# Attention and product-key experts in one kernel: an output-weight load left out at the end, totals stored together, key copies and weight residuals moved to other engines, scores ahead of products

## The chip, the cores and the metric

The kernel runs on one core of a Trainium2 chip, as a single program. The engines are TensorE (PE in the profile, with weight loads as PEld), VectorE (DVE), ScalarE (ACT), GpSimd (POOL) and SyncE (SP); SP does no arithmetic here and issues most of the transfers. Each engine works through its own instructions in order, and waits at semaphores for the others. The metric is the device time of one execution in microseconds (us).

## The reference

With 2048 tokens of width 512, the output is `x + A(xn) + B(xn)`, where `xn` is the layer norm of `x`:

```python
def _A_ref(x, wq, wk, wv, wo):          # 32 query heads of width 16, one key and one value head
    q = (x @ wq).reshape(B, S, H, Dh)   # then heads first
    k, v = x @ wk, x @ wv
    p = softmax(einsum("bhqd,bkd->bhqk", q, k) * Dh ** -0.5)
    return einsum("bhqk,bkd->bhqd", p, v) ... @ wo

def _B_ref(x, w_q, k1, k2, u, v):       # 32 heads, 64 x 64 = 4096 experts, K = 2
    q1, q2 = halves of einsum("nd,dhc->nhc", xf, w_q)
    s1, s2 = q1 @ k1.T, q2 @ k2.T       # 64 scores each
    # top 2 of each, the 4 sums, the best 2 of these: experts and softmax gates g
    act = gelu(einsum("nd,nhkd->nhk", xf, u[top_e]))
    return einsum("nhk,nhk,nhkd->nd", g, act, v[top_e])
```

## The kernel before

**Tiling.** Tokens lie in 16 tiles of 128, four tiles to a group, four groups (0 to 3). Matrix products that must be exact to about fp32 use two-part operands: a rounded high part and a residual (`TERMS`, three matmuls for each product).

**The start** (`project_kv`, `project_q` and what calls them, lines 1183 to 1233). SP loads the first group's `x`, the query weights `wq` (L1187), the first expert weights (L469) and the next groups' `x` (L141, tile `xp`). For each group: VectorE takes means and variances (`norm_group`, L148 to L165, with a square root on ACT at L153), TensorE transposes (L180), ACT copies the high part out of PSUM (L181) and VectorE subtracts for the residual (L182). `wqs` holds the query weights' two parts: ACT makes the high part (L1202), GpSimd the residual (L1203). `project_kv` gives keys and values (L198), copied by ACT (L201), split by VectorE (L203, L204); the keys go into `kaug` at two base partitions, six small transfers for each group (L207 to L209) on ACT's queue. `project_q` makes four blocks of queries for each group (L227): ACT takes the high part (L231), VectorE the residual (L232), ACT the square (L234), TensorE a sum over heads (L235), and SP stores both parts to DRAM (L237, L238). The query parts have four buffers, so a new one waits for an older one's store.

Among this stand the first items of the expert scores: `wp_make` folds the experts' query weights with the key tables (products `pw`, L485; copies L486; transposes `pwt`, L492; copies and residuals L494, L495), and `item` multiplies them with the tokens (`psc`, L530: 12 matmuls for each token tile); VectorE finds maxima and their places (L543, L545), and `batch` turns four tiles' results into expert numbers and gates (L570 to L607, an exponential on ACT at L582). `gathers` then has GpSimd fetch the experts' rows (L964). The order in this part is made by a planner, which takes the program's order and its own durations. The start ends with a flag (`guard`, L262) that every engine reads before a branch.

**The main loop** (lines 1235 to 1306) has its order written out by hand. It runs 280 steps, `d` from 0 to 279, with `i = 2 * d`; 512 attention steps lie in the first 256, and the rest finishes what is under way. A step (`att_steps`) takes scores of one 128-key block against 4 heads (L325), the exponential on ACT (L328) into `pt`, and the products with the values two blocks later (L339). Between these, `run_scores` feeds in pieces of the expert scores up to a budget (`spent` counts their cost; a product `pw` counts 0.9), VectorE makes dot products with gathered rows (`dot`, L976) and weighted sums into `xa` (`add`, L1011). Groups 2 and 3 take the experts densely (`dense`: L723, L807, L848, L851). At step 0 `run_scores` runs first, with a budget of 6.0, which covers the whole of `wp_make`.

**The end.** `experts_out` puts a finished total's store on SP's list, one in each step (L1291, L1292), for the store at L448. `load_wo` loads the output weights into two gather buffers: at L1177 for each 128 steps, and at step 502 for the last block. The last block's attention output goes through `last_out_a` and `last_out_b` (L407, L415), is added to the totals that were read back (L418) and stored from SP and ACT (L419).

```python
        if i >= 128 and i % 128 == 10 or i == STEPS - 10:      # L1177
            load_wo()
```

Of the kernel before, what the change touches and what calls it, by code (L numbers as in the profile page):

```python
# [18 lines left out]
OP = mybir.AluOpType  # L19
# [10 lines left out]
NT = S // P  # L30
# [10 lines left out]
NGB = 12  # L41
# [14 lines left out]
def tile_kernel(ctx, tc, x, wq, wkv, wo, wqT, kT, uv, ub, vb, out):  # L56
    nc = tc.nc
# [11 lines left out]
    raw = lambda ap: ap.bitcast(F32)  # L69
# [122 lines left out]
    def project_kv(g):  # L192
        p = stile("pkv")[:, 0, :]
        n = 0
        for k in range(KC):
            for a, b in TERMS:
                w = (wkv_h, wkv_l)[a]
                nc.tensor.matmul(p[:32, :], w[:, k, :], XT[g][k][:, b, :], start=n == 0, stop=n == 11)  # L198
                n += 1
        kv = big.tile([32, 512], F32, name="kv", tag="wk", bufs=NWK)  # L200
        nc.scalar.copy(kv, p[:32, :])  # L201
        kh = big.tile([32, 2, 512], F32R, name="kh", tag="wk", bufs=NWK)
        nc.vector.tensor_copy(kh[:, 0, :], kv)  # L203
        nc.vector.tensor_tensor(out=kh[:, 1, :], in0=kv, in1=kh[:, 0, :], op=OP.subtract)  # L204
        c = slice(g * 512, (g + 1) * 512)
        for base in (0, 64):
            nc.scalar.dma_start(raw(kaug[base:base + 16, c]), raw(kh[:16, 0, :]))  # L207
            nc.scalar.dma_start(raw(kaug[base + 16:base + 32, c]), raw(kh[:16, 1, :]))
            nc.scalar.dma_start(raw(kaug[base + 32:base + 48, c]), raw(kh[:16, 0, :]))  # L209
        sq = start.tile([16, 512], BF16, name="ksq", tag="sq", bufs=2)  # L210
        nc.vector.tensor_mul(sq, kv[:16, :], kv[:16, :])
        nc.tensor.matmul(ksq_p[32 * g:32 * g + 32, :], blk[:16, 0:1].to_broadcast([16, 32]), sq,
                         start=True, stop=True)
        pt = xtile("pv_t")
        for c in range(GT):
            nc.tensor.transpose(pt[:, 32 * c:32 * c + 32], kv[:, c * P:(c + 1) * P], ident[:32, :32])
        nc.vector.tensor_copy(vaug[:, GT * g:GT * g + GT, :DH],
                              pt[:, :P].rearrange("p (c n) -> p c n", n=32)[:, :, DH:])
# [799 lines left out]
    def gathers(most):  # L1018
        while g_next[0] < NSL and g_next[0] < a_next[0] + NGB - lent[0] and most > 0:
            gather(g_next[0])  # L1020
            g_next[0] += 1
            most -= 1
# [107 lines left out]
    def att_steps(d, mid, fill):  # L1130
        i = 2 * d
        run(STORES)
        if 144 <= i < STEPS and i % 128 == 16:
            PWO.extend((i // 128 - 1, j) for j in range(4))
        if i < STEPS:
            u, kc = divmod(i, 16)
            if i == 0:
                load_q(0, rows=False)
                run_scores(until=spent[0] + 6.0)
            if kc == 4 and u + 1 < 32:  # L1140
                load_q(u + 1)
            scores(u, kc, 0)
            scores(u, kc, 1)
        if 0 < i <= STEPS:
            pu, pk = divmod(i - 2, 16)
            pv(pu, pk)
            pv(pu, pk + 1)
            if pk == 14:
                unit_tail(pu)
        mid()  # L1150
        if i < STEPS:
            scores(u, kc + 1, 0)
            scores(u, kc + 1, 1)
        if out_ready() and (i % 128 >= HOLD and PWO[0][0] != 1 or i % 4 == 0 and PWO[0][0] == 1):
            block_out()
            spent[0] += 3.6
        fill()

        pp, r = divmod(i, 32)
        if pp and pp < 16:  # L1160
            if r == 4:
                pair_load(pp - 1)
            if r == 6:
                pair_invert(pp - 1)
            if r == 10:
                pair_spread(pp - 1)
            if r == 12:
                pair_tail(pp - 1)
        if i == STEPS - 4:
            for j in range(3):  # L1170
                last_out_a(j)
        if i == STEPS + 2:
            last_out_a(3)
            last_out_b()
        if i >= 124 and i % 128 == 124 or i == STEPS - 30:
            lent[0] = 2
        if i >= 128 and i % 128 == 10 or i == STEPS - 10:  # L1177
            load_wo()
        if i == STEPS - 6:
            load_last()  # L1180
# [18 lines left out]
    for i in range(2):  # L1199
        for k in range(2):  # L1200
            w = start.tile([P, 2, 512], F32R, name="wqs", tag="wqs", bufs=4)
            nc.scalar.copy(w[:, 0, :], wraws[i][:, k, :])  # L1202
            nc.gpsimd.tensor_tensor(out=w[:, 1, :], in0=wraws[i][:, k, :], in1=w[:, 0, :], op=OP.subtract)  # L1203
            wqs.append(w)
    project_kv(0)
    norm_group(1, xs[1])
# [11 lines left out]
    transpose_group(2)  # L1218
    project_kv(2)
    xs.append([load_x(3 * GT + j, False) for j in range(GT)])  # L1220
    gathers(NGB)
    project_q(2, wqs)
    norm_group(3, xs[3])
    transpose_group(3)
    project_kv(3)
    project_q(3, wqs)
    run(STORES)
    start_stack.close()
# [6 lines left out]
    with tc.manual_schedule(engines={E_.PE, E_.Activation, E_.DVE, E_.Pool, E_.SP}):  # L1235
# [3 lines left out]
        for d in range(half + 24):  # L1239
# [11 lines left out]
            def mid():  # L1251
# [26 lines left out]
                def go():  # L1278
# [9 lines left out]
                        if rest:  # L1288
                            rest.pop(0)()
                    gathers(4)  # L1290
                    if OUTS:  # L1291
                        experts_out(OUTS.pop(0))  # L1292

                if dense_on[0] == 2:
                    POST_FILL.append(go)
# [58 lines left out]
```

## Time and profile before

| | |
|---|---|
| three timed runs | 1969.92, 1976.40 and 1984.79 us (median 1976.4) |
| the profiled execution's own time | 1972.45 us |
| its span, first to last instruction | 1970.7 us |
| mean granted TensorE clock | 0.975 |
| moved by DMA | 492.16 MB, mean 250 GB/s |
| software (gather) queue, share of 16 DMA engines | 41.2% |
| SP's and ACT's queues, share | 34.0% and 0.3% |

The page gives each engine's busy time over the span, with idle time put down to what ended it. An idle engine that nobody waits for costs nothing, so the busy shares say where to look, and the stretch at hand says what an edit is worth. Three kinds of rows are used below. A row of stretches has the stretch, its length, busy time and instruction count of PE, PEld, DVE, ACT and POOL, the granted clock, the DMA engines' share and GB/s. A row in order of time has start, length, engine, line, operation, output and inputs, and in brackets the idle time before it and what ended that. A row of waits has who waited for whom, us in total, how often, and the longest.

### The profile page before, as it was taken

The page shows a single profiled execution, that of the slowest core. Times are in us where ns is not written, and L with a number is a line of the kernel's source. Part 1 is how long each engine was busy: PE and PEld are TensorE (multiplying, and loading weights), DVE is VectorE, ACT ScalarE, POOL GpSimd, SP SyncE. Part 2 cuts the span into 40 slices and gives each one's busy share as a digit, 9 for nine tenths or more (in the row PEclk, how much of TensorE's full clock was granted, in tenths as well). Part 3 has the DMA queues.
Part 4 walks back from the last instruction along what each step waited for, and adds up shares of the span by engine and source line. Part 5 has one row for each costly group of instructions (what it writes and reads, how often), then busy time and mean ns, then how long its engine had stood idle before and what let it go on. Part 6 is the DMA issues. An engine that isn't in the chain of part 4 may idle for free.

```text
span 1970.7 us, 34755 instructions
## 1 busy us (share of the span) xinstructions
PE 1874.1 (95%) x10990; PEld 998.1 (51%) x10990; DVE 1679.4 (85%) x6713; ACT 1292.3 (66%) x1801; POOL 575.1 (29%) x540
## 2 busy tenths in 40 slices
PE   6879999999999998999999999999999989999997
PEld 3544444555555443555555445555554545555552
DVE  6626888899999975899999789999999769999993
ACT  3326666655557885788778555555578767778773
POOL 2201323222221222344344332222213215444430
PEclk9989999999999898999999999999999899999999
DMA  7756878787773676698889978877646858899982
GB/s 271 281 202 223 297 267 287 274 297 259 249 229 119 214 227 211 211 291 290 273 277 306 351 271 275 277 237 260 204 135 227 267 169 277 278 286 279 294 265 80
DMA packets 234201, 492.16 MB, mean 250 GB/s; under 512 B 93204, under 2 KB 93460, under 8 KB 234012
## 3 DMA queue, kind: packets, MB, share of 16 engines
q0 software_dynamic: 73728, 268.47, 41.2%
q1 hardware_dynamic: 158280, 219.82, 34.0%
q10 hardware_dynamic: 2004, 1.61, 0.3%
q8 instruction: 88, 1.44, 0.3%
q14 instruction: 101, 0.83, 0.1%
HBM read 428.46 MB, written 56.07 MB: 246 GB/s over the span
## 4 chain that ended last, share of the span: by engine, by line
PE 65%; DVE 18%; DMA 4%; ACT 2%; issue 2%; SPq 1%; another core or an unknown queue 0%; ACTq 0%; DVEq 0%
PE pv L339 18%; PE sc L325 13%; PE psc L530 10%; PE pout L848 9%; PE pact L723 9%; DVE i L545 5%; DVE m L543 3%; DVE xa L1011 3%; PE pg L807 3%; DVE g L976 2%; ACT pt L328 2%; PE pw L485 1%; PE pwo L432 1%; DMA dg<-gst 1%; DMA wqt<-in_wqT_dram 1%
## 5 line engine op out<-in xcount | busy, mean ns | idle before, releaser
L328 ACT ACTIVATE pt<-sc 128x1024 f32<-128x1024 f32 x1024 | 993.2, 1025 | 461.3 <-PE sc L325 392.6
L964 POOL DMA_INDIRECT g<-in_uv_dram,idx x512 | 561.9, 1097 | 1333.1 <-DVE xa L1011 724.1
L339 PE MATMUL pv<-pt,vaug 128*32 128x512 f32 x4096 | 511.1, 617 | 0.0
L325 PE MATMUL sc<-qa,kaug 64*128 64x512 f32 x2048 | 389.0, 454 | 26.6 <-ACT pt L328 25.8
L530 PE MATMUL psc<-wk,xt 128*128 128x512 f32 x1536 | 391.3, 402 | 5.9 <-DMA wk<-dw 2.1
L1011 DVE SCALAR_TENSOR_TENSOR xa<-g,w,xa 128x512 f32<-128x512 f32 x512 | 374.0, 750 | 0.1
L976 DVE CUSTOM_DVE_ANT_0 g<-g,xa 128x512 f32<-128x512 f32 x512 | 337.0, 687 | 7.4 <-DMA g<-in_uv_dram,idx 7.4
L530 PEld LDWEIGHTS psc<-wk,xt 128*128 128x128 f32 x1536 | 279.3, 189 | 110.7 <-issue 42.6
L325 PEld LDWEIGHTS sc<-qa,kaug 64*128 64x128 f32 x2048 | 157.6, 186 | 347.9 <-ACT pt L328 225.2
L339 PEld LDWEIGHTS pv<-pt,vaug 128*32 128x32 f32 x4096 | 109.2, 111 | 255.4 <-issue 253.8
L545 DVE FIND_INDEX8 i<-m,psc 128x8 uint32<-128x64 f32 x1024 | 207.5, 231 | 0.0
L723 PE MATMUL pact<-xt,wk 128*128 128x512 f32 x768 | 197.6, 402 | 1.0 <-DVE i L545 1.0
L848 PE MATMUL pout<-wk,wd 128*128 128x512 f32 x768 | 194.9, 402 | 0.2 <-DVE wd L906 0.2
L723 PEld LDWEIGHTS pact<-xt,wk 128*128 128x128 f32 x768 | 140.0, 189 | 50.3 <-issue 17.7
L848 PEld LDWEIGHTS pout<-wk,wd 128*128 128x128 f32 x768 | 140.8, 188 | 47.4 <-DVE act L976 5.1
L543 DVE MAX8 m<-psc 128x8 f32<-128x64 f32 x1024 | 146.8, 220 | 18.2 <-PE psc L530 16.6
L688 DVE TENSOR_TENSOR wk<-rw,wk 128x512 fp32r<-128x512 f32 x128 | 85.5, 688 | 9.1 <-ACT wk L687 9.1
L851 DVE TENSOR_TENSOR da<-da,pout 128x512 f32<-128x512 f32 x128 | 83.2, 684 | 10.2 <-PE pout L848 10.1
L545 DVE MATCH_VALUE_LOAD i<-m,psc 128x8 f32 x1024 | 81.5, 80 | 0.0
L773 DVE TENSOR_TENSOR oh<-oh 128x2048 f16<-128x2048 f16 x64 | 78.1, 1220 | 0.0
L999 DVE SCALAR_TENSOR_TENSOR w<-gth,ga 128x4 f32<-128x4 f32 x128 | 20.6, 161 | 66.3 <-ACT gth L992 65.6
L687 ACT CAST wk<-rw 128x512 fp32r<-128x512 f32 x128 | 74.0, 629 | 3.2 <-DMA rw<-in_ub_dram 3.1
(155 smaller groups left out, 1350.0 us busy)
## 6 DMA issues: line engine op xcount, KB each, us to landing
wk<-dw SPq DMA_DIRECT2D x96, 512.0 KB
wqt<-in_wqT_dram SPq DMA_DIRECT2D x32, 512.0 KB
dw<-wk SPq DMA_DIRECT2D x32, 512.0 KB
rw<-in_ub_dram SPq DMA_DIRECT2D x64, 256.0 KB
rw<-in_vb_dram SPq DMA_DIRECT2D x64, 256.0 KB
gy<-dg SPq DMA_DIRECT2D x64, 256.0 KB
dg<-gst SPq DMA_DIRECT2D x30, 512.0 KB
qa<-dqh SPq DMA_DIRECT2D x128, 64.0 KB
```

The lines of the kernel that those rows point to most:

```text
L325: nc.tensor.matmul(p[:, b, :], kaug[o:o + 64, kc * P:(kc + 1) * P], QA[u][o:o + 64, i, :], start=True, stop=True)
L328: nc.scalar.activation(pt, p, AF.Exp, scale=SCALE)
L339: nc.tensor.matmul(PV[u][32 * j:32 * j + 32, :], vaug[:, kc, :], pt[:, b, :], start=kc == 0, stop=kc == 15)
L530: nc.tensor.matmul(p, XT[g][k][:, a, j * P:(j + 1) * P], WC[n_][k][:, bb, :], start=n == 0, stop=n == 11)
L543: nc.vector.max(m8[:, jb, s, :], p[:, s * E:(s + 1) * E])
L545: nc.vector.max_index(i8[:, jb, s, :], m8[:, jb, s, :], p[:, s * E:(s + 1) * E])
L688: behind(lambda: nc.vector.tensor_tensor(out=w[:, 1, :], in0=rw[:, i, :], in1=w[:, 0, :], op=OP.subtract))
L723: nc.tensor.matmul(p, us[:, a, k * P:(k + 1) * P], XT[DG][k][:, c, :], start=n == 0, stop=n == 11)
L848: nc.tensor.matmul(p, wd[0][:, a, j * P:(j + 1) * P], vs[:, c, :], start=n == 0, stop=n == 5)
L964: nc.gpsimd.indirect_dma_start(out=gt, out_offset=None, in_=uv, in_offset=bass.IndirectOffsetOnAxis(ap=IDX[ph, c, ti][:, s:s + 1], axis=0))
L976: nc.vector.tensor_tensor_reduce(u, u, XN[TPH * ph + ti], scale=1.0, scalar=0.0, op0=OP.mult, op1=OP.add, accum_out=a[:, i:i + 1])
L1011: nc.vector.scalar_tensor_tensor(acc, v, w[:, i:i + 1], acc, op0=OP.mult, op1=OP.add)
```

## The change

Seven edits. The key copies move from ACT's queue to SP's. The query weights' residual is made by VectorE instead of GpSimd. The twelve gathers before the loop are asked for in two halves, the second after the last group's keys. The loop's first `run_scores` gets a budget of 1.8 instead of 6.0, so that the first attention scores stand ahead of the rest of `wp_make`'s products. The output weights' load is limited to steps below 512, which leaves out the one at step 522. In the last steps (from `d` = 252 on) all finished totals are stored at once instead of one in each step. The arithmetic is the same.

```diff
@@ project_kv
         for base in (0, 64):
-            nc.scalar.dma_start(raw(kaug[base:base + 16, c]), raw(kh[:16, 0, :]))
-            nc.scalar.dma_start(raw(kaug[base + 16:base + 32, c]), raw(kh[:16, 1, :]))
-            nc.scalar.dma_start(raw(kaug[base + 32:base + 48, c]), raw(kh[:16, 0, :]))
+            nc.sync.dma_start(raw(kaug[base:base + 16, c]), raw(kh[:16, 0, :]))
+            nc.sync.dma_start(raw(kaug[base + 16:base + 32, c]), raw(kh[:16, 1, :]))
+            nc.sync.dma_start(raw(kaug[base + 32:base + 48, c]), raw(kh[:16, 0, :]))
@@ att_steps
             if i == 0:
                 load_q(0, rows=False)
-                run_scores(until=spent[0] + 6.0)
+                run_scores(until=spent[0] + 1.8)
...
-        if i >= 128 and i % 128 == 10 or i == STEPS - 10:
+        if 128 <= i < STEPS and i % 128 == 10 or i == STEPS - 10:
             load_wo()
@@ the start
             nc.scalar.copy(w[:, 0, :], wraws[i][:, k, :])
-            nc.gpsimd.tensor_tensor(out=w[:, 1, :], in0=wraws[i][:, k, :], in1=w[:, 0, :], op=OP.subtract)
+            nc.vector.tensor_tensor(out=w[:, 1, :], in0=wraws[i][:, k, :], in1=w[:, 0, :], op=OP.subtract)
...
-    gathers(NGB)
+    gathers(NGB // 2)
     project_q(2, wqs)
     norm_group(3, xs[3])
     transpose_group(3)
     project_kv(3)
+    gathers(NGB // 2)
     project_q(3, wqs)
@@ the main loop, mid()
                     gathers(4)
-                    if OUTS:
-                        experts_out(OUTS.pop(0))
+
+                    for _ in range(1 if d < half - 4 else NT):
+                        if OUTS:
+                            experts_out(OUTS.pop(0))
```

## The prediction

> **What bounds the kernel now.** I read the page first, then busy time by stretches, then the order of time in the three stretches that the diff touches: the start (to the branch at 136 us), the first steps of the main loop, and the end.
>
> ```profile
> span 1970.7 us, 34755 instructions
> PE 1874.1 (95%) x10990; PEld 998.1 (51%) x10990; DVE 1679.4 (85%) x6713; ACT 1292.3 (66%) x1801; POOL 575.1 (29%) x540
> PE 65%; DVE 18%; DMA 4%; ACT 2%; issue 2%; SPq 1%; another core or an unknown queue 0%; ACTq 0%; DVEq 0%
> ```
> ```profile
> core 0: us, PE busy (x) PEld busy (x) DVE busy (x) ACT busy (x) POOL busy (x), PEclk, DMA share, GB/s
> 0.00:136.00 136.00, 99.24 (x424) 65.22 (x426) 75.28 (x247) 40.71 (x72) 25.12 (x40) 0.95 0.72 258
> 136.00:160.00 24.00, 18.96 (x70) 6.97 (x70) 6.03 (x17) 11.60 (x16) 0.00 (x0) 0.72 0.63 215
> 160.00:1935.00 1775.00, 1733.55 (x10428) 917.99 (x10426) 1590.87 (x6437) 1233.61 (x1707) 549.94 (x500) 0.98 0.77 253
> 1935.00:1971.00 36.00, 22.40 (x75) 7.89 (x72) 7.19 (x12) 6.40 (x7) 0.00 (x0) 0.88 0.29 95
> ```
> ```profile
> 0.00:18.00 18.00, 2.49 (x9) 1.67 (x10) 11.13 (x20) 4.16 (x7) 13.19 (x28) 1.00 0.92 319
> 59.00:73.00 14.00, 14.00 (x62) 11.16 (x63) 13.44 (x104) 1.62 (x4) 0.00 (x0) 1.00 0.65 234
> 84.00:93.00 9.00, 5.49 (x16) 3.43 (x15) 1.84 (x4) 0.58 (x1) 5.17 (x5) 0.73 1.03 420
> ```
>
> From 160 to 1935 us TensorE is busy 1733.6 of 1775 us: there the order on TensorE is the time. In the order of the two built programs that stretch is the same on every engine, so what the ends gain or lose shifts it and should not change it. At the ends nothing is full: TensorE idles 36.8 us in the start, 5 us in the loop's first 24 us (at a granted clock of 0.72) and 13.6 us in the last 36. So the change is worth what it takes out of chains of waits there.
>
> **The end: output weights and totals.** The loop runs some steps past the last score; one of them matches the load's condition once more, and two loads of 512 KB go out that nobody reads.
>
> ```profile
> 1932.59 1.41 DVE L1011 SCALAR_TENSOR_TENSOR xa<-g,w,xa 128x512 f32<-128x512 f32 x2
> ...
> 1959.34 1.53 SPq L419 DMA_DIRECT2D out_dram<-ft  x2
> 1959.94 1.76 ACTq L419 DMA_DIRECT2D out_dram<-ft  x2
> ...
> 1962.58 1.95 SPq L399 DMA_DIRECT2D wo<-in_wo_dram  x2
> ```
> ```profile
> SPq L1350 <- DMA wo<-in_wo_dram: 4.5, 1, 4.5
> ```
> ```profile
> 1951.75 1.99 DMA rsb<-e
> ```
>
> The last real store is issued by 1961.70 (1959.94 + 1.76), but the closing wait holds another 4.5 us after the loads' issue ends at 1964.53, to about 1969.3, and 1.4 us later the span ends. Without them the last store is what ends it: a small transfer lands in 1.99 us, a 256 KB one, by estimate, up to 0.8 us later (its bytes at the 319 GB/s of the first row above), so 1963.7 to 1964.5, and with the 1.4 us of closing 1965.1 to 1965.9. The totals that SP now stores behind the final sums (three of six sit there) go out ahead of them; the last add that feeds them ended at 1934.00, 16 us before SP's next work, so they hold nobody up, and they stop sharing the DMA engines with the final stores. I take **−5.5 us**, bounds −4.5 and −6.
>
> **Start, query weights.** Four subtractions leave GpSimd for VectorE.
>
> ```profile
> 10.12 5.30 POOL L1203 TENSOR_TENSOR wqs<-g,wqs 128x512 fp32r<-128x512 f32 x4 [2.49 <-ACT wqs L1202]
> ```
> ```profile
> L165 DVE TENSOR_SCALAR xa<-xa,mv,rs 128x512 f32<-128x512 f32 x4 | 5.6, 1458 | 0.0
> L162 DVE TENSOR_TENSOR rs<-rs,y 128x4 f32<-128x4 f32 x1 | 1.2, 1175 | 0.0
> ```
> ```profile
> L165 DVE TENSOR_SCALAR xp<-xp,mv,rs 128x512 f32<-128x512 f32 x8 | 3.8, 543 | 0.1
> ```
> ```profile
> 8.02 13.55 SPq L141 DMA_DIRECT2D xp<-in_x_dram  x8
> ```
>
> While GpSimd subtracts, the same normalising step takes 1458 ns instead of 543, and L162 1.2 us: VectorE loses 3.7 + 1.0 us. Four subtractions on VectorE cost 4 x 688 ns (the like instruction, L688 on the page: "85.5, 688") = 2.8 us. That would be −1.9 us; but in the new order the first residuals stand behind the statistics of the second group's first tile, whose load is issued at 8.02 behind 4 MB of others, and 4.2 MB at 319 GB/s take some 13 us from the first loads on, so by estimate it lands at 14 to 17 us, about when VectorE gets to it. So it is hidden between **0 and −1.9 us**; I take −0.5.
>
> **Start, key copies.** Each group sends six small copies from ACT's queue.
>
> ```profile
> L207 ACTq DMA_DIRECT2D kaug<-kh x8: 514/597/1015, 25.5 to 114.4; - x8
> ```
> ```profile
> PE pqs L235 <- ACT qsq L234: 9.7, 8, 2.0
> ACT kv L201 <- remote: 5.7, 1, 5.7
> ACT qt L231 <- DVE vaug L217: 5.1, 1, 5.1
> ACT wt L486 <- DVE st L148: 4.3, 1, 4.3
> ACT qt L231 <- DMA kaug<-kh: 4.3, 1, 4.3
> ```
>
> Six issues of 0.6 us hold ACT 3.6 us and more; the last three rows are three of these blocks (the named releaser had long been done), together 13.7 us. Most of that TensorE covers with the next product in its other PSUM buffer; what it does not cover shows in the first row: 9.7 us in eight waits for ACT's squares, of which those of the blocked groups go, and those that VectorE causes stay. On SP, which has 81 transfers in the start, 24 more stand in order ahead of the query stores, and wait there for VectorE's key halves; behind them queue the stores that free the four query buffers. I take half of the 9.7, **−5**, bounds −9.7 and 0.
>
> **Start, scores ahead of products.** With other durations and the gathers split in two halves, the planner sets the start anew. Ahead of the first 48 score matmuls stand 9 of the second group's projection matmuls instead of 25; the others, the statistics of the last group and two dot products of the main loop come later.
>
> ```profile
> 70.52 5.52 PE L227 MATMUL pq<-xtt,wqs 128*128 128x512 f32 x23
> ```
> ```profile
> 75.36 1.28 ACT L582 ACT_TABLE_LOAD   x1
> 76.66 0.22 ACT L582 ACTIVATE ex<-mx 128x16 f32<-128x16 f32 x1
> ```
> ```profile
> 84.15 0.94 POOL L964 DMA_INDIRECT g<-in_uv_dram,idx  x1 [0.30 <-DMA g<-in_uv_dram,idx]
> ```
>
> Sixteen matmuls at 5.52/23 = 0.24 us bring the scores 3.8 us forward, and with them the stretch in which VectorE is full (13.44 of 14 us); the projections then run on TensorE under it. Against that, after the scores VectorE has four statistics of 0.66 us, two dot products of 0.69 (page, L976: 687) and ACT a table load of 1.28, since a square root now stands behind the exponential: 2.6 + 1.4 + 1.3 = 5.3 us in a serial stretch, and the dots wait for gathers, in whose stretch the DMA engines are full (1.03 at 420 GB/s). The net of these is between +4 and −6. The 5.7 us of ACT in the last list is a stall in that full stretch that no row explains; whether it comes again I leave open, in these bounds. I take **−3.5**.
>
> The Trainium skill, "ScalarE: Activation LUTs", section "What ACT_TABLE_LOAD costs", prices each change of table set at 1283 ns plus a drain of about 1380 ns. The rows show 1.28 us and the exponential 0.02 us behind it; by the page's figure the two extra loads (the second stands ahead of the loop's first exponential) would cost 2.8 us more than by the row, and the sum would be −14.7 instead of −17.5.
>
> **First steps of the loop.**
>
> ```profile
> 135.89 3.60 PE L485 MATMUL pw<-wqt,kTs 128*64 128x512 f32 x8 [5.42 <-PEq L264]
> 140.74 1.08 PE L485 MATMUL pw<-wqt,kTs 128*64 128x512 f32 x4 [1.25 <-issue]
> 142.90 1.98 PE L485 MATMUL pw<-wqt,kTs 128*64 128x512 f32 x4 [1.08 <-DMA wqt<-in_wqT_dram]
> ```
> ```profile
> 149.61 5.68 ACT L328 ACTIVATE pt<-sc 128x1024 f32<-128x1024 f32 x6 [0.90 <-PE sc L325]
> ```
> ```profile
> 160.17 1.08 PE L485 MATMUL pw<-wqt,kTs 128*64 128x512 f32 x4
> ```
>
> Before, all four products, 16 transposes and 3 matmuls stand ahead of the first attention scores; after, three products do, and the rest is dealt out between the exponentials. The first scores can start at 141.8 (140.74 + 1.08) instead of 148.9, so the exponentials start 7.1 us earlier less the second table load, 1.3. From the matmuls at 160.17 on both orders are one again, so only the time to there counts: of the 24.3 us, eight exponentials (0.95 us each) and 19.0 us of TensorE work must still fit. TensorE's idle 5 us is what can go; −6 if the clock also rises, +1 if the copies between the exponentials hold up the next scores. I take **−3**.
>
> **Sum.** −5.5 − 0.5 − 5 − 3.5 − 3 = −17.5 us, on the profiled execution's 1972.45 us (span 1970.7) 1955. The three timed runs were 1969.92 to 1984.79; with the profiled one their middle is 1974.4, so I forecast 1957 us.
>
> **The rivals.** *The whole gain of the start comes through.* The copies at 7, the reordering at its −6, the loop's start at −4: −6 − 1.9 − 7 − 6 − 4 = −24.9, 1950. For it: every one of these waits is on the chain between two groups; against: VectorE's extra 5.3 us.
>
> *TensorE keeps its clock.* 18.96 us of matmuls ran at a granted 0.72 in the loop's first 24 us; at full clock they take 13.7, another −5.3 us: 1952. The half-clock windows follow stretches with idle TensorE (0.73 at 84 to 93), and fewer gaps remain. But the last gap, from the flag to the branch, stays. The Trainium skill, "TensorE: Matmul & The Clock Gate", section "What's actually happening", has the clock halve after an idle window of some 3.4 us and return after as long a busy one; by that rule the branch alone makes the loop start at half clock, and the gain would be lost. The trace agrees: 0.72 there.
>
> *Only the end gains.* SP's longer queue and the dots give the start's savings back: −5.5 to −8, 1967.
>
> *SP becomes the start's limit.* The eight loads at 8.02 took 13.55 us to issue because each waited for an earlier transfer to land, 1.7 us apiece. If the 24 key copies each waited like that in order, 41 us of SP time would stand ahead of the query stores. It decides against the change once more than the forecast's 17.5 us of it reach TensorE: with half, 1957 + 5 (the copies' gain undone) + 20.5, near 1983. Against it: in the built programs the copies on ACT already wait for the same earlier transfers, and a small one lands in about 2 us.
>
> *The change doesn't do what it says* can't be for the loads, whose two instructions are gone from SP's order.
>
> **How the numbers follow.** Within 1% is about what a measurement of this kernel can tell from no change; faster by more means under 1956.6, right beside the forecast. Forecast as summed 0.40, nearly all within 1%; whole gain 0.25 and clock 0.12, both faster; only the end 0.16, within; SP as limit 0.07, slower in most. The forecast's scatter puts 0.05 of it on the faster side: faster 0.42, same 0.52, slower 0.06. The likeliest is the forecast, 1957. The range reaches down to the whole gain with scatter (1944) and up to the end alone (1970), which leaves out SP as limit and the far tails.
>
> **What would show it.** The closing wait on SP ends on a store, some 3 us after the last add, and no transfer of output weights follows it: the end. The blocks of 4 to 5 us before ACT's copies in the start are gone, and the branch comes near 127 us instead of 136: the start. From the branch to the first exponential under 9 us instead of 14: the loop's first steps. The stretch between keeps its 1775 us within the scatter. I would be wrong if that stretch changed by more than 10 us, if VectorE's first dot waited several us for its gather with residuals behind it, or if SP's waits for key halves showed up as waits of ACT for query buffers.

## The result, and the profile after

The changed kernel takes 1961.34 us in the middle of 20 runs (1951.51 to 1970.41), the kernel before 1971.39 (20 runs, 1963.81 to 1984.79): a ratio of 0.9944, 95% interval 0.9928 to 0.9961. The two middles lie 10 us apart; the ratio is 11 us of the kernel before's time. That is within 1%, as forecast, but 7 us short of the 17.5 us that the sum had. The pair of profiles shows the whole 17.9 us (spans 1970.7 and 1952.8), so the first question is where 8 us went between the profiles and the runs. A part of the answer is luck: the profiled execution of the changed kernel, 1954.53 us, is its second shortest of 20, and that of the kernel before, 1972.45 us, is 1 us longer than its middle.

The page of the kernel after, its head and its chain:

```profile
span 1952.8 us, 34758 instructions
PE 1868.9 (96%) x10990; PEld 995.7 (51%) x10990; DVE 1675.6 (86%) x6717; ACT 1294.1 (66%) x1803; POOL 566.5 (29%) x536
PE 62%; DVE 22%; DMA 5%; ACT 2%; issue 1%; SPq 1%; DVEq 0%; ACTq 0%
```

Its busy time by the same four stretches as before (to the branch; to the point from which both orders are one; the loop; the end):

```profile
0.00:128.70 128.70, 97.66 (x422) 64.34 (x423) 73.15 (x255) 42.10 (x73) 19.65 (x36) 0.96 0.77 272
128.70:149.70 21.00, 15.57 (x70) 6.17 (x70) 4.64 (x12) 13.27 (x17) 0.00 (x0) 0.85 0.48 167
149.70:1923.40 1773.70, 1733.22 (x10427) 917.49 (x10426) 1590.61 (x6439) 1232.35 (x1706) 546.86 (x500) 0.98 0.77 254
1923.40:1952.80 29.40, 22.46 (x76) 7.72 (x72) 7.19 (x12) 6.40 (x7) 0.00 (x0) 0.91 0.16 53
```

The start is 7.2 us shorter (the branch's first product at 128.71, not 135.89), the next stretch 3.3, the loop 1.1, the end 6.3. The end is as clean as a profile gets. In order of time, and by SP's waits:

```profile
1948.30 1.79 ACTq L419 DMA_DIRECT2D out_dram<-ft  x2
1949.03 0.69 DVE L418 TENSOR_TENSOR ft<-ft,pwl 128x512 f32<-128x512 f32 x1 [0.16 <-PE pwl L415]
```
```profile
SPq L1353 <- DMA out_dram<-ft: 1.9, 3, 0.7
```

The last add ends at 1949.72 and the span 3.1 us later, on a store; before, 9.4 us lay there.

In the start the gain does not stand still. Rows in order of time of the kernel after:

```profile
51.00 11.09 PE L530 MATMUL psc<-wk,xt 128*128 128x512 f32 x48
61.93 3.60 PE L227 MATMUL pq<-xtt,wqs 128*128 128x512 f32 x15
...
74.47 0.69 DVE L976 CUSTOM_DVE_ANT_0 g<-g,xa 128x512 f32<-128x512 f32 x1 [4.11 <-DMA g<-in_uv_dram,idx]
...
85.77 0.58 ACT L201 COPY kv<-pkv 32x512 f32<-32x512 f32 x1 [2.23 <-PE pkv L198]
...
106.69 0.57 ACT L201 COPY kv<-pkv 32x512 f32<-32x512 f32 x1 [1.51 <-PE pkv L198]
```

The first scores come 8.2 us sooner (59.23 before), the third group's keys 1.7 (87.50), the fourth group's 4.8 (111.48). VectorE waits 4.1 us for gathered rows with a query residual queued behind, which the prediction had named as a sign against itself.

All profiles side by side; the kernels between before and after, and below them, are those of the next section. "Scores" is the first L530 product, "third" and "fourth" the groups' L201 copy, "branch" the first product behind it, "common" the matmuls from which all orders are one, "loop" from the first value product behind that to the first of the last block's output products (L407), "tail" from the last add to the end of the span; all in us, of one profiled execution each. Then the middle of the timed runs (20 of after, 9 of copies_alone, 6 of gathers_behind, 12 of each other) and the ratio to the kernel before, run on the same chip. The kernel before had its middle at 1970.2 to 1972.0 us there, so the ratio isn't that of two rows of this table.

| kernel | scores | third | fourth | branch | common | loop | tail | runs | ratio (95%) |
|---|---|---|---|---|---|---|---|---|---|
| before | 59.2 | 87.5 | 111.5 | 135.9 | 160.2 | 1773.3 | 9.4 | 1971.4 | 1 |
| b_end | 58.8 | 83.3 | 110.5 | 134.9 | 155.1 | 1771.2 | 3.1 | 1967.8 | 0.9990 (0.9967-1.0013) |
| b_weights | 57.2 | 83.2 | 110.4 | 134.5 | 158.6 | 1777.9 | 9.5 | 1972.6 | 1.0004 (0.9979-1.0029) |
| b_scores | 58.0 | 82.5 | 111.0 | 135.5 | 158.0 | 1770.7 | 9.3 | 1968.0 | 1.0005 (0.9979-1.0032) |
| b_keys | 56.6 | 87.6 | 114.6 | 136.7 | 160.9 | 1771.9 | 9.4 | 1973.3 | 1.0034 (1.0012-1.0056) |
| keys_weights | 52.8 | 81.9 | 109.5 | 132.3 | 156.7 | 1766.9 | 8.9 | 1967.3 | 0.9987 (0.9966-1.0008) |
| start_only | 52.4 | 88.4 | 109.3 | 131.6 | 152.7 | 1779.5 | 9.3 | 1967.5 | 0.9973 (0.9948-0.9999) |
| after | 51.0 | 85.8 | 106.7 | 128.7 | 149.7 | 1772.2 | 3.1 | 1961.3 | 0.9944 (0.9928-0.9961) |
| dots_behind | 52.6 | 81.9 | 109.3 | 131.9 | 155.1 | 1779.4 | 3.1 | 1964.9 | 0.9966 (0.9947-0.9984) |
| order_alone | 52.0 | 86.1 | 109.5 | 133.4 | 154.4 | 1771.2 | 3.1 | 1964.5 | 0.9966 (0.9946-0.9986) |
| copies_alone | 56.3 | 85.5 | 110.6 | 133.0 | 154.1 | 1768.5 | 3.1 | 1959.6 | 0.9941 (0.9918-0.9964) |
| gathers_held | 52.7 | 87.8 | 108.0 | 134.8 | 157.8 | 1772.5 | 3.1 | 1962.3 | 0.9957 (0.9935-0.9980) |
| gathers_late | 52.2 | 81.3 | 101.2 | 125.4 | 153.7 | 1780.3 | 3.1 | 1963.4 | 0.9948 (0.9930-0.9966) |
| gathers_behind | 53.0 | 82.2 | 102.0 | 124.6 | 147.7 | 1780.6 | 3.1 | 1957.3 | 0.9915 (0.9888-0.9943) |

How to read it: the tail hardly scatters. The branch of kernels with the same instructions up to it scatters by 1 us before (135.9 and 134.9) and by 3 after (128.7 and 131.6, start_only); of these 3 us, 1.4 stand already at the first group's keys (22.7 and 24.1). The loop, whose instructions are the same in all but the last three, runs from 1766.9 to 1779.5 us with no order in it. A difference of two single profiles therefore carries several us of chance; here it made 10 us look like 18.

### The profile page after: what moved, and what is told of

It reads as the page before. It is cut to its first block, busy times and chain, and to the rows that moved or that the text cites. A ratio compares the mean times of both kernels' runs of the same rounds, so it can differ in the third digit from the quotient of the medians.

```text
span 1952.8 us, 34758 instructions
## 1 busy us (share of the span) xinstructions
PE 1868.9 (96%) x10990; PEld 995.7 (51%) x10990; DVE 1675.6 (86%) x6717; ACT 1294.1 (66%) x1803; POOL 566.5 (29%) x536
## 4 chain that ended last, share of the span: by engine, by line
PE 62%; DVE 22%; DMA 5%; ACT 2%; issue 1%; SPq 1%; DVEq 0%; ACTq 0%
PE pv L339 17%; PE sc L325 12%; PE psc L530 10%; PE pout L848 9%; PE pact L723 9%; DVE i L545 5%; DVE xa L1011 4%; DVE m L543 3%; DVE g L976 3%; PE pg L807 2%; DVE oh L773 1%; ACT pt L328 1%; PE pw L485 1%; PE pwo L432 1%; DMA dg<-gst 1%
## 5 line engine op out<-in xcount | busy, mean ns | idle before, releaser
L530 PE MATMUL psc<-wk,xt 128*128 128x512 f32 x1536 | 390.8, 402 | 7.1 <-DVE wk L495 3.5
L530 PEld LDWEIGHTS psc<-wk,xt 128*128 128x128 f32 x1536 | 278.7, 189 | 112.0 <-issue 39.3
L807 PEld LDWEIGHTS <-oh 128*128 128x128 f16 x1024 | 68.5, 164 | 15.4 <-issue 7.3
```

Of the source, the lines that this page charges most:

```text
L530: nc.tensor.matmul(p, XT[g][k][:, a, j * P:(j + 1) * P], WC[n_][k][:, bb, :], start=n == 0, stop=n == 11)
L807: nc.tensor.matmul(p[:, i * NB:(i + 1) * NB], oa[:, :, i], ob[:, :, i], start=True, stop=True)
```

## The experiments

**The parts alone, on the kernel before.** The key copies on SP's queue:

```diff
-            nc.scalar.dma_start(raw(kaug[base:base + 16, c]), raw(kh[:16, 0, :]))
+            nc.sync.dma_start(raw(kaug[base:base + 16, c]), raw(kh[:16, 0, :]))
...
```

> The kernel before with only the key copies on SP's queue. Built, this alone already moves 16 projection matmuls behind the first scores (57 instead of 73 stand ahead); no dot products stand ahead of the branch. Theory A (each part is worth what the checkpoints of the two profiles show, and the rest of the kernel keeps its length): from the second group's keys on, the groups come 2.8, 3.1 and 2.2 us sooner each, and the stretch after the scores loses little, because the 4.1 us wait for gathered rows isn't there: the branch falls from 136 to 126-129 us and the time by 7 to 9 us. Theory B (what the start gains, the loop takes back): the branch comes as early, but the time falls by less than 3 us. Theory C (the copies were hidden anyway): the branch stays within 2 us of 136.

The branch came at 136.7 us and the runs were 0.34% longer. A is out, C holds for the branch. Since the edit also moves the 16 matmuls, it tests the new queue and the new order as one. The waits between 74 and 113 us, first of b_end, which has the old start and where ACT issues the copies, then of b_keys:

```profile
ACT qt L231 <- DMA kaug<-kh: 8.4, 1, 8.4
```
```profile
ACT qt L231 <- DMA dqh<-qt: 9.3, 1, 9.3
```

ACT no longer waits for its own copies, but for a query buffer whose store stands behind the copies on SP. Such a wait is not the mark of SP's copies alone: in b_weights and b_scores, where ACT issues the copies, there is one of 6.4 and 6.0 us beside the waits for the copies. SP's issues and ACT's query copies of b_keys in order of time:

```profile
91.35 0.58 SPq L207 DMA_DIRECT2D kaug<-kh  x1
...
91.46 0.59 ACT L231 CAST qt<-pq 128x512 fp32r<-128x512 f32 x1 [3.32 <-PE pq L227]
...
93.29 0.51 SPq L208 DMA_DIRECT2D kaug<-kh  x1
95.77 0.51 SPq L209 DMA_DIRECT2D kaug<-kh  x1
98.33 0.33 SPq L237 DMA_DIRECT2D dqh<-qt  x1
...
105.99 0.58 ACT L231 CAST qt<-pq 128x512 fp32r<-128x512 f32 x1 [9.29 <-DMA dqh<-qt]
```

The first block of the third group's queries was ready at 92.05 (91.46 + 0.59), but its store was issued at 98.33, because the transfers ahead of it could go only one in 1.9 to 2.6 us, and ACT got the buffer for the third block at 105.99. The stretches 75 to 102 us of b_keys show why (the last two columns are the DMA engines' share and GB/s):

```profile
75.00:84.00 9.00, 6.44 (x29) 4.21 (x29) 4.20 (x13) 4.62 (x8) 6.37 (x8) 1.00 1.04 357
84.00:93.00 9.00, 9.00 (x44) 6.13 (x44) 6.41 (x14) 2.53 (x5) 2.80 (x3) 1.00 1.03 399
93.00:102.00 9.00, 8.61 (x39) 6.13 (x39) 0.69 (x1) 1.59 (x3) 0.00 (x0) 1.00 1.03 404
```

The twelve gathers go out from 72.0 to 88.0 us and the DMA engines are full for 27 us. Whatever is issued in that time waits, on whichever queue.

The first allowance cut to 1.8:

```diff
-                run_scores(until=spent[0] + 6.0)
+                run_scores(until=spent[0] + 1.8)
```

> The kernel before with only the planner's first allowance cut from 6.0 to 1.8. Built, this alone puts two dot products ahead of the branch and deals the loop's first products out between the attention scores; the 73 projection matmuls ahead of the first scores stay. Theory A: the start is 0 to 4 us longer by the dot products' wait for gathered rows (branch at 136-140 us), and from the branch to the common point it takes 21.0 instead of 24.3 us: time between -3.3 and +1 us. Theory B: the wait is hidden in the stall that ACT has there anyway, and the loop takes the 3.3 us back: within 1 us of no change.

Branch at 135.5, where the old start has 135.9 and 134.9, so no cost of the dot products can be seen there; 22.6 us to the common point, more than A's 21.0; and 1.0005 in the runs. Neither theory is told from the other by that interval of 5 us to both sides.

The two edits of the end (the load's condition and the totals' loop, as in the diff above):

> The kernel before with only the two edits of the end: no last load of output weights, and the done totals stored at once. Theory A: from the last add to the end of the span 3.1 instead of 9.4 us, all of it seen in the time: -6 us. Theory B (the end's gain is partly the profile's): less than 4 us in the timed runs.

The tail is 3.1 us, A's number exactly. The two edits ran only together, so how the 6.2 us divide between the loads left out and the totals stored sooner is not shown. The runs gave 2.4 us, and the interval reaches from 6.5 us faster to 2.6 slower: by itself this tells nothing. Between start_only and after, which differ by the end alone, it is 0.9973 against 0.9944, some 5.7 us, but these intervals overlap too. So the runs are compatible with 6.2 us, and no more is settled.

The weight residuals on VectorE:

```diff
-            nc.gpsimd.tensor_tensor(out=w[:, 1, :], in0=wraws[i][:, k, :], in1=w[:, 0, :], op=OP.subtract)
+            nc.vector.tensor_tensor(out=w[:, 1, :], in0=wraws[i][:, k, :], in1=w[:, 0, :], op=OP.subtract)
```

> The kernel before with only the four residuals of the query weights on VectorE. Theory A: the first group's keys and values come 1.6 us sooner (22.7 instead of 24.3 us) and the branch with them: -1.6 us. Theory B (a wait behind it takes it up): the branch within 0.5 us of 136, no change that can be measured.

The first group's keys came later in this profile, not sooner (25.3 against 23.0 to 24.3 in before, b_end and b_scores, which have the old start), the second group's 0.6 to 1.9 us sooner (44.3 against 44.9 to 46.1), the third's as in b_end and b_scores. The branch, at 134.5, lies 0.4 us ahead of the old start's earliest; so A's way is out, and the runs show no change, as B said, though B's 136 was missed by more than its half us.

**Parts together.** No part of the start gains alone, so they were put together: keys and weights, and then the whole change without the end.

```diff
+        if i >= 128 and i % 128 == 10 or i == STEPS - 10:
...
+                    if OUTS:
+                        experts_out(OUTS.pop(0))
```

These lines of the kernel before stand in the second of the two, start_only, in place of the new ones.

> The kernel before with two parts together: key copies on SP and the weight residuals on VectorE. Theory A (in the start, the stretch in which the twelve gathers fill the DMA engines sets the end; what is issued in it, key copies or query stores, waits there for its place, so that the copies alone only changed ACT's wait of 8.4 us for its copies into one of 9.3 us for query buffers; a part gains only where it brings the scores, and so the gathers, forward): both together bring the first scores from 56.6 (keys alone) to 51-53 us and the first gather from 72.0 to 66-68, SP's wait for places shrinks, and the branch comes at 127-131 us. Theory B (the parts add up as they did alone, +1 and -1 us at the branch): the branch at 134-137 us.

> The kernel after with the end as before: the last load of output weights is back and the totals go out one at a time. Theory A (the start's parts gain together, 7 us at the branch and 3 behind it): 4 to 7 us faster than before in the timed runs, and slower than the kernel after by the 3 to 6 us of the end. Theory B (the start gains nothing in the timed runs): within 2 us of before.

With keys and weights the scores came at 52.8, the first gather at 68.2 and the branch at 132.3: closer to A than to B, but short of A's range, and ACT still waits 9.9 us for a query buffer. The whole start gives 131.6 and 0.9973, 4 us in the middle of the runs: A's lower edge. Its branch, 131.6 and not 128.7, is what shows that the profile of the kernel after had 3 us of luck in the start.

**Dot products.** Only the allowance differs from the kernel after.

```diff
-                run_scores(until=spent[0] + 1.8)
+                run_scores(until=spent[0] + 4.2)
```

> The kernel after with the planner's first allowance at 4.2 instead of 1.8. Built, this alone puts the two dot products back behind the branch; the loop's first scores then stand behind all projections of the first units and 8 transposes. Theory A (the dot products' 4.1 us wait for gathered rows held the residuals and with them the third group): kv of the third group at 81-83 instead of 85.8 us, branch at 125-127 instead of 128.7, the common point of the loop within 1 us of the kernel after, since the loop's front is a little later again. Theory B (the wait is covered by the full DMA engines, whose stores hold the third group anyway): branch at 128-130 us and the common point 1 to 3 us later than in the kernel after.

A's first sign came, and what should have followed didn't. Against start_only, which has the same instructions up to the dot products, the third group's keys come 6.5 us sooner, at 81.9; but the fourth group's come at 109.3 in both, the branch is 0.2 us later and the common point 2.4. That is B's account; B's range for the branch, 128 to 130, was set by the one profile of the kernel after and is missed by 2 us. Without the 4 us wait for gathered rows ACT waits 10.0 us for a query buffer instead of 2.6. The wait for rows was only a part of the wait for the buffer.

**Gathers.** In the kernel after the second six gathers are asked for later, but nothing holds GpSimd back: they follow the first six at once, twelve from 66.4 to 81.6 us. Here they are held by a write into their buffers:

```diff
         gt = gtile()
+        if 6 <= m < NGB:
+            nc.gpsimd.tensor_tensor(out=gt[:, :32], in0=vaug[:, 12, :32], in1=vaug[:, 12, :32], op=OP.add)
         nc.gpsimd.indirect_dma_start(
```

> The kernel after with the second six gathers really held back: GpSimd first writes 32 columns of each of their buffers from the last group's values, so that they go out only behind that group's keys (about 107 us), and not at once as in both kernels; the gather then overwrites these columns. Built, this also keeps the two dot products behind the branch. Theory A (the gathers' full DMA stretch sets the start): the stretch with full DMA engines falls from about 18 us to under 10, the waits for query buffers and key copies in the third and fourth group go, and the branch comes at 120-125 instead of 128.7 us; 3 to 6 us faster than the kernel after unless the six late gathers hold up the loop's first dot products. Theory B (the start is bound by the chain through ACT and VectorE): branch within 2 us of 127, which is the kernel after without the dot products' wait, and no gain in the time.

The branch came at 134.8: neither. The expectation was wrong in one thing, the dot products still stood ahead of the branch (4.7 us of waiting, third group at 87.8); and the six gathers, from 110.5 on, filled the DMA engines to 0.90 under the last group's query stores, where the fourth group took 22.0 us from its keys to the flag instead of 17.5. The next kernel mends both.

```diff
+        if 6 <= m < NGB:
+            nc.gpsimd.tensor_tensor(out=gt[:, :1], in0=qmax[:, 3:4], in1=qmax[:, 3:4], op=OP.add)
...
-                run_scores(until=spent[0] + 1.8)
+                run_scores(until=spent[0] + 3.8)
...
-    gathers(NGB // 2)
     project_q(3, wqs)
+    gathers(NGB // 2)
```

> The kernel after with the second six gathers held until the last group's query maxima are there (about 122 us; one column of each buffer is written by GpSimd from the maxima and then overwritten by the gather), and the planner's first allowance at 3.8, which puts the dot products behind the branch; in the run with the gathers held to the last group's keys they still stood ahead of it. Theory A (the stretch with full DMA engines sets the third group's pace, whoever waits in it): the third group's keys at 82 us, no wait for query buffers over 4 us, the fourth group's keys at 102-105 instead of 107-109, the branch at 123-127 instead of 129-132 us; 3 to 6 us of it reach the time unless the late gathers delay the loads behind the branch, which would show as a first product later than 5 us after the flag or a common point more than 23 us behind the branch. Theory B (ACT and VectorE set the pace): branch at 129-132 us and the time of the kernel after.

A, with its exception. The fourth group's keys come at 101.2 (109.3 in dots_behind, which has the dot products behind the branch too), no wait for a query buffer is over 3.4 us, the branch falls to 125.4; and then the common point is 28.3 us behind it, and the time is that of the kernel after. SP's loads of the factored query weights behind the branch, in gathers_late and, further below, in gathers_behind:

```profile
125.51 10.74 SPq L469 DMA_DIRECT2D wqt<-in_wqT_dram  x4
```

**The order and the queue, apart.** Moving the second group's key copies alone makes the planner move the 16 projection matmuls, so both can be had singly, on the kernel after. In all six copies, for order_alone (copies_alone has `g != 1`):

```diff
-            nc.sync.dma_start(raw(kaug[base:base + 16, c]), raw(kh[:16, 0, :]))
+            (nc.sync if g == 1 else nc.scalar).dma_start(raw(kaug[base:base + 16, c]), raw(kh[:16, 0, :]))
...
```

> The kernel after with only the second group's key copies on SP; those of the other three groups are on ACT again. Built, this keeps the moved order (57 instead of 73 projection matmuls ahead of the first scores). Theory A (the order brings the gain, the queue of the copies only decides who waits): scores at 52-53 us, ACT waits some 8 us for its copies in the third group in place of the query buffers, branch at 130-133 us, time within 2 us of the kernel after. Theory B (the copies off ACT are worth the 5 us of the prediction): branch at 135 us or later, time 3 to 5 us above the kernel after.

> The kernel after with the second group's key copies on ACT and those of the other three on SP. Built, this has the old order (73 projection matmuls ahead of the first scores). Theory A: scores at 55-57 us, gathers 3 to 4 us later than in the kernel after, branch at 133-136 us, time 2 to 4 us above the kernel after. Theory B (the copies are what gains): branch at 129-132 us, time as the kernel after.

Branches at 133.4 and 133.0, ratios whose intervals overlap with each other and with that of the whole change (copies_alone's 0.9941 is as good as the whole's 0.9944): the scores come 4.3 us later in copies_alone, and the branch does not. ACT's wait for its copies is back in order_alone (10.2 us in two), as A said; but neither theory is told from the other, and which of the two is worth more stays open.

**The gathers behind the weight loads.** The second six gathers are held behind the loop's first weight loads; `WC["last"]` is the tile that `wp_load` filled last, and the second call of `gathers` in the start is left out, so that the loop's own calls ask for them:

```diff
+        if NGB // 2 <= m < NGB:
+            lw = WC["last"]
+            nc.gpsimd.tensor_tensor(out=gt[:, :1], in0=lw[:, 0, :1], in1=lw[:, 0, :1], op=OP.add)
...
-                run_scores(until=spent[0] + 1.8)
+                run_scores(until=spent[0] + 3.8)
...
     project_kv(3)
-    gathers(NGB // 2)
```

> The kernel after with the planner's first allowance at 3.8 and the second six gathers held behind the loop's first loads of factored query weights: GpSimd writes one column of each of their buffers from the weights last loaded, and the gather overwrites it. Theory A (the full DMA stretch of twelve gathers is the price of the start, and in the run with late gathers it only moved onto the weight loads behind the branch): the flag at about 119 us as with late gathers, the first product 5 us behind it, not 6.2, the four weight loads issued in 5 to 6 us instead of 10.7, the common point 22-24 us behind the branch (146-149 us), and the time 3 to 5 us below the kernel after, 0.991 to 0.993 of before. Theory B (whoever moves the gathers pays in the next stretch): the loop's first dot products wait for the last gathers, common point at 152 us or later or the loop longer than the 1767-1780 us of the other profiles; time as the kernel after, 0.994 to 0.997 of before.

0.9915 (0.9888 to 0.9943), 1957.3 us in the middle of 6 runs: A, in every place named (flag at 120.0, first product 4.6 us behind it, common point 23.1 behind the branch); of B's signs only the loop is there, by less than 1 us. Stretches 75 to 102 us, and SP's loads:

```profile
75.00:84.00 9.00, 8.12 (x43) 5.15 (x43) 7.16 (x17) 4.85 (x9) 0.73 (x1) 1.00 1.02 388
84.00:93.00 9.00, 8.97 (x37) 6.04 (x36) 2.23 (x5) 2.67 (x5) 0.00 (x0) 1.00 0.89 347
93.00:102.00 9.00, 8.04 (x42) 5.21 (x41) 4.72 (x7) 4.02 (x9) 0.00 (x0) 1.00 0.76 235
```
```profile
125.50 5.36 SPq L469 DMA_DIRECT2D wqt<-in_wqT_dram  x4
```

The DMA engines are full in 9 of the 27 us, the last key copies and query stores find a place, the loads behind the branch take half the time that they took in gathers_late (in the kernel after they took 5.28 us), and the common point is 147.7. The kernel to hold it against is dots_behind, which differs only in asking for all twelve gathers at once and in an allowance of 4.2 instead of 3.8, and has the dot products behind the branch too. The last two of these three stretches in dots_behind:

```profile
84.00:93.00 9.00, 8.97 (x37) 6.03 (x36) 1.97 (x4) 2.37 (x4) 1.00 (x2) 1.00 1.03 420
93.00:102.00 9.00, 2.99 (x18) 2.32 (x16) 0.20 (x1) 1.00 (x3) 0.00 (x0) 0.86 0.90 335
```

TensorE is busy 2.99 of the last 9 us there and 8.04 here; the fourth group's keys and the branch come 7.3 us later there (109.3 and 131.9 against 102.0 and 124.6); and the two ratios, 0.9966 (0.9947 to 0.9984) and 0.9915 (0.9888 to 0.9943), have intervals that don't overlap. This is what shows that the gathers' full DMA stretch holds the start up.

gathers_behind is faster than the kernel before, by 0.6 to 1.1%. That it is faster than the kernel after is not shown: the two were not run on one chip, and the intervals (0.9888 to 0.9943, 0.9928 to 0.9961) overlap a little. Its loop and that of gathers_late, 1780.6 and 1780.3 us, lie just above the others; its profiled execution, 1961.02 us, was the longest of the six, so whether the late gathers cost something there stays open.

## Why the prediction was right, and where not

**The end, -5.5: right.** Six tails with the load are 8.9 to 9.5 us, eight without it 3.1: -6.2, a little past the bound of -6. The closing wait ends on a store. The mis-sized term is that store's landing and the closing: from the end of the last store's issue (1948.30 + 1.79 = 1950.09) to the end of the span it took 2.7 us, where the step had 3.4 to 4.2. The step's "last real store" is that of the final sums; SP issued two totals' stores until 1962.49 in the kernel before, but the change puts them ahead, as the step said.

**Query weights, -0.5: the mechanism right, the size too small to tell.** Without GpSimd beside it VectorE takes 1.91 us for the four normalising steps instead of 5.59, and then waits for the second group's first tile, whose statistics start at 15.9 us in b_weights and 16.0 in the kernel after: inside the step's 14 to 17. The first group's keys come at 22.7 to 25.3 us in the kernels with the edit and at 23.0 to 24.3 in those without, so nothing can be told there, and the runs of b_weights show no change. Together with the key copies the residuals bring the scores from 56.6 to 52.8.

**Key copies, -5: wrong.** The step took half of TensorE's 9.7 us of waits for ACT's squares as what the copies off ACT would free. In the kernel after the same row, up to 130 us, is hardly smaller:

```profile
PE pqs L235 <- ACT qsq L234: 8.9, 6, 3.1
```

Nor do these waits set the branch: in dots_behind they are down to 4.1 us, and the branch is at 131.9. Alone the copies moved the branch by about +1 us (136.7 against 135.9 and 134.9) and the runs by +0.34%. With the residuals on VectorE they gained 2.2 us at the branch (134.5 in b_weights, 132.3 in keys_weights), which is within the scatter of single profiles. The step had the queue right, "behind them queue the stores that free the four query buffers", but priced the move by ACT's issue time and waits, not by the place in time: the third group's copies fall into the 27 us in which the gathers hold the DMA engines full. ACT's waits for query buffers are the sign that the prediction named for being wrong: 9.3 us in b_keys, 3.2 in the kernel after.

**Scores ahead of products, -3.5: the 3.8 us were right, what followed was not.** With the residuals on VectorE too, the kernels with the moved order have the scores at 52.0 to 53.0 (51.0 in the profile after), those with the old order at 56.3 (copies_alone) and 57.2 (b_weights); with the residuals on GpSimd the moved order has 56.6 and the old one 58.0 to 59.2. The projections do run under VectorE's full stretch, as the step said: on TensorE 15 of them stand from 61.93 to 65.53, and VectorE is busy from 53.96 to 70.36 us. But the gain isn't kept, because the third and fourth group wait for the same DMA stretch as before: start_only and dots_behind reach the fourth group's keys at 109.3, only 1 us ahead of b_end and b_weights. Of the extra 5.3 us of serial work the dot products and their wait were not the price, since taking them out changed the branch by 0.2 us; the statistics and the table load were not taken out. Nor did splitting the gathers in the program split them on GpSimd.

**First steps, -3: the size was right, the reason only in part.** Length to the common point and granted clock, from the rows of before, b_end, start_only and b_scores:

```profile
135.90:160.10 24.20, 19.16 (x70) 7.08 (x70) 6.03 (x17) 11.70 (x16) 0.00 (x0) 0.72 0.63 213
```
```profile
134.90:155.10 20.20, 16.46 (x70) 5.96 (x70) 6.03 (x17) 11.13 (x16) 0.00 (x0) 0.81 0.74 256
```
```profile
131.60:152.70 21.10, 15.59 (x72) 6.15 (x72) 4.67 (x12) 13.22 (x17) 0.00 (x0) 0.85 0.49 166
```
```profile
135.40:158.00 22.60, 18.95 (x70) 6.89 (x70) 4.63 (x12) 12.11 (x16) 0.00 (x0) 0.64 0.43 155
```

The old order at 0.81 takes 20.2 us, less than the new order at 0.85; at 0.67 to 0.72 it takes 24.1 to 24.4, the new one at 0.64 22.6. By these few rows the new order is some 1.5 us better at a low clock and not better at a high one, and the rest of the 3.3 us is clock. But the order may bring the clock too: the new one had 0.83 to 0.85 in four of six kernels, the old one 0.67 to 0.72 in four of five, and the runs don't part the two. Over all of them the means are 21.6 and 23.4 us. The sign that the prediction named is there: the first exponential stands 7.5 us behind the branch (136.19 and 128.71), not 14. The clock's share is the rival "TensorE keeps its clock", in part: 0.85, not 1.

**The sum.** With the sizes measured more than once: the start -4.7 (the mean of after, start_only and dots_behind, 130.7, against that of before and b_end, 135.4), the first steps 0 to -1.8, the end -6.2: -10.9 to -12.7, where the runs have -10 to -11 (-7.7 to -14.2 by the interval). The forecast's -9 for the start is the term that was too large, by some 4 us; how that divides between the copies and the reordering is not shown: order_alone and copies_alone, each with the one in the main and not the other, have the branch at 133.4 and 133.0. That the time was forecast so well is partly luck: 1957 was reckoned from 1974.4 us, the middle of four executions, and the kernel before has 1971.4 over 20, which hid 3 us of the error. The range, 1944 to 1970, also holds the rival in which only the end gains, so the time alone doesn't bear out the steps of the start. The gain of the start did not vanish in the loop (1772.2 against 1773.3 in the pair, no order in the others); on average it was smaller than the pair shows. The rival with SP as the limit named the right queue and the right mechanism, but 1.9 to 2.6 us a copy for the last of one group's copies, not 1.7 us for 24: it costs the gain of the copies, not 20 us.

## What to carry to other kernels

Before pricing a transfer's move from one queue to another, look at the DMA share of the stretch into which it falls: here, at 1.03, the new queue only changed who waited, and what gained was to move the gathers that fill the engines, to a stretch behind the next urgent loads. A request that is split in the program goes out in one piece if nothing holds its engine back, as the twelve gathers did. And a difference of single profiles should be checked part by part against a second profile with the same instructions, since here the like parts differed by up to 5 us (the third group's keys at 82.5 to 87.5 in before, b_end and b_scores).

## What the runs showed of the hardware

A short wait can cost twice. In the kernel after TensorE waited 2.33 us for `wqt` from 227.6 us on; at the same place of the kernel before, in order of time:

```profile
238.74 1.08 PE L485 MATMUL pw<-wqt,kTs 128*64 128x512 f32 x4 [0.82 <-DMA wqt<-in_wqT_dram]
239.75 1.65 PE L530 MATMUL psc<-wk,xt 128*128 128x512 f32 x6
```

and of the kernel after, in order of time and by stretches:

```profile
229.91 1.24 PE L485 MATMUL pw<-wqt,kTs 128*64 128x512 f32 x4 [2.33 <-DMA wqt<-in_wqT_dram]
231.08 2.93 PE L530 MATMUL psc<-wk,xt 128*128 128x512 f32 x6
```
```profile
223.40:230.50 7.10, 4.77 (x32) 1.69 (x31) 4.85 (x20) 4.07 (x6) 2.14 (x2) 1.00 0.84 297
230.50:237.50 7.00, 7.00 (x34) 2.80 (x30) 3.45 (x27) 2.96 (x4) 0.93 (x1) 0.76 0.74 273
237.50:244.50 7.00, 7.00 (x48) 3.88 (x44) 4.95 (x32) 4.62 (x7) 0.94 (x1) 1.00 0.44 153
```
```profile
231.10:231.70 0.60, 0.60 (x4) 0.50 (x3) 0.00 (x0) 0.51 (x1) 0.40 (x1) 0.50 0.50 174
```

The six matmuls behind the wait take 2.93 us instead of 1.65. Cut into such short pieces, the stretch has a granted clock of 0.50 from 231.1 to 234.0 us, with a part of it just before and behind. The wait took 1.5 us more than in the kernel before, and the slow clock behind it another 1.5. The Trainium skill, "TensorE: Matmul & The Clock Gate", section "What's actually happening", has the clock fall after at least one idle window of about 3.4 us, in windows that run freely. The slow stretch is as long as the page's window, a loss of 0.24 of 7 us being 3.4 us at half clock, but here 2.33 us of idle time were enough to bring it about.

The scatter of the runs goes with the clock: of the kernel after, the run at a mean clock of 0.982 took 1951.51 us, the one at 0.971 took 1970.41, with the others between in nearly that order.

The two extra table loads cost what their rows say. In ACT's order of time of the kernel after:

```profile
76.42 1.28 ACT L153 ACT_TABLE_LOAD   x1
77.71 0.21 ACT L153 ACTIVATE sd<-ve 128x4 f32<-128x4 f32 x1
...
134.30 0.59 ACT L486 COPY wt<-pw 128x512 f32<-128x512 f32 x1 [1.56 <-PE pw L485]
134.90 1.28 ACT L328 ACT_TABLE_LOAD   x1
136.19 3.77 ACT L328 ACTIVATE pt<-sc 128x1024 f32<-128x1024 f32 x4
```

The load at 134.90 stands 0.01 us behind the copy and 0.01 us ahead of the exponential: the drain of some 1380 ns that the Trainium skill adds ("ScalarE: Activation LUTs", section "What ACT_TABLE_LOAD costs") shows on neither side, and the measurement decides.
